# Routing attention and a tanh-shrink layer on one core: half of the first batch's up-projection in products of quarters

## The chip, the core and the metric

The kernel runs on one core of a Trainium2 chip. A core has a matmul engine (TensorE, "PE" in the profile, its weight loads "PEld"), a vector engine (VectorE, "DVE"), an activation engine (ScalarE, "ACT"), a general engine (GpSimd, "POOL") and a queue that only issues transfers (SyncE, "SP"). Each works through its own instructions in the order written and waits on semaphores. The metric is device time in microseconds, the median of several executions.

## The reference

Attention with routing: every query and key is assigned to the nearest of 16 centroids of its head, and a query sees only the keys of its own cluster. Then a two-layer block with the activation h - tanh(h).

```python
q, k, v: (4, 8, 768, 64)    centroids: (8, 16, 64)    w_in: (512, 2048)    w_out: (2048, 512)

q_assign = argmax(q_n . c_n)           k_assign = argmax(k_n . c_n)
mask   = q_assign[..., :, None] == k_assign[..., None, :]
scores = where(mask, q k^T / sqrt(64), -1e9)
attn   = softmax(scores)
x      = (attn v) as (4 * 768, 512)
h      = x @ w_in
out    = (h - tanh(h)) @ w_out
```

## The kernel before, in words

Everything is f32. Heads go in pairs (128 rows); a pair has two halves of 384 queries, and each half three steps of 256 keys. The list `steps` (L971) orders this work, 96 steps for 16 pairs: steps 0 to 11 are the first halves of batch 0's four pairs, 12 to 23 their second halves, and from 24 on come the pairs of batches 1 to 3 with both halves together, 24 steps (2 x HALF, HALF = 12) for a batch.

The main loop (L1103) writes one step after the other. For a step it emits the score matmuls of the step after (`begin`, L443; exps on ScalarE), the value matmuls of the step itself (`value`, L498) and some items of a "fill", the matmuls of the two-layer block of an earlier batch. What other engines have to do is kept in a list `todo`, and `between()` spreads it over the slots after the fill's items: the masks (`select`, L475: VectorE multiplies the exps by "key's cluster equals query's cluster", four operations, and POOL adds the weights up for the softmax's divisor, two operations of 128x768), the stages of a later pair (`turns`: transposes; `similar`; `route`, L358: the nearest centroid; `publish`: codes to DRAM), the chain that divides (`total`, `compact`, `invert`, `spread_out`, `scale`) and the makers.

A fill's items carry a weight, and the loop takes as many in each step as the weight's share of the fill's steps allows. Batch 0 is projected by `plain_items` (L665): first half in steps 12 to 23, second half in 24 to 47. For one half the up-projection has 16 items (`up`, L669, weight 2.6), each one chunk of 128 rows of h: 4 chunks of x times 2 half-widths of weights, 384 columns; ScalarE takes tanh from PSUM, VectorE subtracts. Then 12 items of the down-projection (`project`, L687, weight 3.4). An f32 product stands as two matmul instructions in the profile, so an item of `up` has 16.

Batches 1 to 3 use Strassen's scheme in Winograd's form (`strassen_items`, L834): x and the weights are cut into quarters, and 7 products of half the depth take the place of 8. The weights' seven combinations ("factors") are made once by `up_maker` and `down_maker` (L730, L751): sums on VectorE, then writes to DRAM by SP (`up_factors`, `down_factors`). The makers run as 44 entries of todo in steps 26 to 46. Factors come back as `stream` tiles of about 0.9 MB, three buffers, by `fetch_factors` (L786), two ahead. The combinations of x are made by `right_factors` (L822), 8 operations on VectorE for a batch, with 384 columns. Each of the 56 up-products (`up_product`, L840) is 8 matmul instructions on a PSUM tile of 384 columns; VectorE adds the products up to the quarters of h, then tanh on ScalarE and the subtraction on POOL (`shrink`).

PSUM tiles of the tag "f" (products, routing, divisors) share three buffers in turn. The weights w_in lie in a pool of their own on the right side of SBUF; `open_stream` (L799, at step 39) gives that place to the stream tiles and to a "den" tile, and `open_late` (L810, at step 48) gives the first batch's other tiles to the rest.

Of the kernel before, what the change touches and what calls it, by code (L numbers as in the profile page):

```python
# [39 lines left out]
P = 128  # L40
# [18 lines left out]
def kernel(  # L59
# [119 lines left out]
    def fast():  # L179
# [178 lines left out]
        def route(n: int):  # L358

            t = sims.pop(n)  # L360
            ps = ps_f.tile([P, TB], F32, name="pr", tag="f")
            for j in range(HCH):
                c = slice(j * P, (j + 1) * P)
                nc.tensor.transpose(out=ps[:, c], in_=t[:, c], identity=ident)  # L364
            G = HCH * 8
            pr = ps.rearrange("p (g c) -> p g c", c=C)
            shape = [P, G, C]
            places = down.unsqueeze(1).to_broadcast(shape)
            mx = rtp.tile([P, G], F32, name="mx")
            nc.vector.reduce_max(out=mx, in_=pr, axis=AX.X)  # L370
            top = rtp.tile(shape, F32, name="top")
            nc.vector.tensor_tensor(  # L372
                out=top, in0=pr, in1=mx.unsqueeze(2).to_broadcast(shape), op=ALU.is_ge
            )
            nc.vector.tensor_tensor(out=top, in0=top, in1=places, op=ALU.mult)
            code = codes[n] = codep.tile([P, 2, 2, 2, HCH], F32, name="code")
            nc.vector.reduce_max(
                out=code.rearrange("p i a h j -> p j (i a h)"),
                in_=top.rearrange("p (j g) c -> p j g c", j=HCH), axis=AX.X,
            )  # L380
# [238 lines left out]
        def spread_out(n: int, half: int):  # L619
            back = lists.pop((n, half))  # L620
            if joined(n):
                pool = late_pools.get("den", sump)
                dens[n, 1] = pool.tile([P, TB], F32, name="den")
                for i in range(2):
                    for h in range(2):
                        nc.sync.dma_start(
                            dens[n, i][h * D : h * D + D], back[i, h : h + 1].to_broadcast([D, TB])
                        )
                return
            for h in range(2):  # L630
                nc.sync.dma_start(
                    dens[n, half][h * D : h * D + D], back[h : h + 1].to_broadcast([D, TB])
                )
# [31 lines left out]
        def plain_items(half: int):  # L665
# [39 lines left out]
            if half == 0:  # L705

                order = [(s, i) for i in range(NQ4) for s in range(2)] + order[2 * NQ4 :]
            return [(2.6, 1, lambda between, f=f: up(f, between)) for f in sequence] + [
                (3.4, 1, lambda between, s=s, i=i: project(s, i, between)) for s, i in order
# [76 lines left out]
        def fetch_factors(n: int):  # L786

            if n < (B - 1) * PER:
                i = n % PER
# [7 lines left out]
        late_pools, diffs = {}, {}  # L797

        def open_stream():  # L799
# [4 lines left out]
            late_pools["den"] = cx.enter_context(  # L804
                tc.tile_pool(name="den_late", bufs=1, side="right", reuse_waits="tile")
            )
            for n in range(2):
                fetch_factors(n)

        def open_late():  # L810
            first.close()
            for name, bufs in (
                ("diff", 1), ("u", 2), ("s", 2), ("th", 2), ("g", 1), ("left", 1), ("du", 1),
                ("c", 4), ("raw", 2),
# [6 lines left out]

        def right_factors(b: int, c: int):  # L822

            if c == 0:
                diffs[b] = late_pools["diff"].tile([P, 3, CH, TB], F32, name="diff")
            d = diffs[b]
            x, y = xT[b * HP + c], xT[b * HP + CH + c]
# [6 lines left out]
        def strassen_items(b: int):  # L834
            base = (b - 1) * PER

            held = {}
            G, left1 = late_pools["G"], late_pools["S1"]

            def up_product(i: int, k_: int, between):  # L840
                which = PRODUCTS[k_]
                x = [xT[b * HP + c] for c in range(CD)]
                d = diffs[b]
                right = {
                    1: [x[c][:, 0] for c in range(CH)], 2: [x[CH + c][:, 0] for c in range(CH)],
                    3: [x[CH + c][:, 1] for c in range(CH)], 4: [d[:, 2, c] for c in range(CH)],
                    5: [d[:, 0, c] for c in range(CH)], 6: [d[:, 1, c] for c in range(CH)],
                    7: [x[c][:, 1] for c in range(CH)],
                }[which]
                if k_ == 0:  # L850
                    held[i] = (
                        late_pools["s"].tile([P, TB], F32, name="s"),
                        late_pools["u"].tile([P, 2, TB], F32, name="u"),
                    )
                s, u = held[i]
                g = G[:, i]
# [4 lines left out]
                def shrink(f: int, halves_=slice(0, 2)):  # L861
                    t = g[:, f, halves_]
                    th = late_pools["th"].tile([P, 2, TB], F32, name="th")[:, halves_]
                    nc.scalar.activation(out=th, in_=t, func=ACT.Tanh)  # L864
                    t, th = (x.rearrange("p a n -> p (a n)") for x in (t, th))
                    nc.gpsimd.tensor_tensor(out=t, in0=t, in1=th, op=ALU.subtract)  # L866

                ps = ps_f.tile([P, TB], F32, name="pu", tag="f")
# [8 lines left out]
                elif which == 2:  # L877
                    add(g[:, 0, 0], ps, s)
                    if i == HF - 1:
                        shrink(0, slice(0, 1))  # L880
# [5 lines left out]
                elif which == 4:  # L886
                    add(g[:, 1, 0], ps, u[:, 1])
                elif which == 5:
                    add(u[:, 0], ps, u[:, 0])
                    add(g[:, 1, 1], ps, u[:, 1])  # L890
                    shrink(1)
                else:
                    add(g[:, 0, 1], ps, u[:, 0])

                    shrink(0, slice(1 if i == HF - 1 else 0, 2))
                between()
                if k_ == len(PRODUCTS) - 1:

                    nc.gpsimd.tensor_tensor(out=left1[:, i], in0=g[:, 0, 1], in1=g[:, 1, 1], op=ALU.add)
                    nc.gpsimd.tensor_tensor(  # L900
                        out=g[:, 0, 1], in0=g[:, 0, 0], in1=g[:, 0, 1], op=ALU.subtract
                    )
                    streams.pop(base + i)
# [3 lines left out]
            def down_product(k_: int, j: int, between):  # L907
# [51 lines left out]

            return [  # L960
                (1.3, 1, lambda between, i=i, k_=k_: up_product(i, k_, between))
                for i in range(HF) for k_ in range(len(PRODUCTS))
            ] + [
# [11 lines left out]
        def before(n: int):  # L975
# [10 lines left out]
            yield lambda: route(n)  # L986
# [7 lines left out]
        ready = {}  # L994
# [68 lines left out]
        route(0)  # L1063
        turn(1, 0, nc.scalar)
# [13 lines left out]
        route(1)  # L1078
        begin(steps[0])
# [23 lines left out]
        for at, (n, half, s) in enumerate(steps):  # L1103
# [4 lines left out]
            if at == 4 * HALF - 9:  # L1108
                open_stream()
            if at in fills:  # L1110
                fill, over = fills[at][0](), fills[at][1]
                whole, spent, since = sum(it[0] for it in fill), 0.0, at
            if at == 2 * HALF:
                makers = [it for i in range(2) for it in up_maker(i)]
                makers += [it for i in range(2) for it in down_maker(i)]
# [71 lines left out]
            todo += [stages[i] for i in (5, 3, 4, 2) if i in stages]  # L1187
            todo += late
# [18 lines left out]
            light = [i for i in range(at, 4 * HALF - 2) if i % 3 and i % 6 != 1]  # L1207
# [8 lines left out]
            slots = max(sum(it[1] for it in now), 1)  # L1216
            place = iter(range(slots))
# [10 lines left out]
            if at in fills and "raw" in late_pools:  # L1228
# [10 lines left out]

        PRS = len(PRODUCTS)  # L1240
        tail = tail[:2] + tail[PRS : PRS + 2] + tail[2:PRS] + tail[PRS + 2 :]
# [218 lines left out]
```

## Time and profile before

| | |
|---|---|
| median of 5 runs | 982.39 us (982.27 to 982.99) |
| the profiled execution | 983.58 us |
| its span, first to last instruction | 981.8 us |
| TensorE busy | 971.4 us, 6456 matmul instructions |
| VectorE, ScalarE, POOL busy | 535.7, 316.5, 497.1 us |
| up-projection of batch 0, both halves (L676) | 86.3 us of TensorE, 512 instructions |
| up-projection of batches 1 to 3 (L871) | 134.9 + 102.3 us, 1344 instructions |
| granted TensorE clock | 1.0 |

Step k is found in the trace by its score matmuls (L451): step 20 begins at 160.1 us, step 24 at 202.4, step 25 at 208.8, step 36 at 288.8. In the page, busy time of PE is the time with at least one matmul in flight; matmuls overlap, so the mean duration of one (487 ns for L676) is longer than what it adds. The chain of work that ended last names, piece by piece, what the run's end waited for.

### The profile page before, as it was taken

What the parts mean: (1) busy time and instruction counts of PE and PEld (TensorE: products, weight loads), DVE (VectorE), ACT (ScalarE), POOL (GpSimd) and SP (SyncE); (2) the same over time, 40 slices, a digit from 0 to 9 for tenths busy, and PEclk for the clock granted to TensorE, in tenths of its full rate; (3) what the DMA queues carried; (4) which work ended last, traced back from release to release, by engine and by line L of the source; (5) the groups of instructions that cost most, each with busy time, mean ns of one, the idle gap of its engine ahead of it and who ended that gap; (6) DMA issues with size and microseconds to landing.
All of it is one profiled execution on the core that took longest, in us unless ns stands there. A gap on an engine that the chain in (4) does not pass through costs nothing.

```text
span 981.8 us, 16550 instructions
## 1 busy us (share of the span) xinstructions
PE 971.4 (99%) x6456; PEld 460.2 (47%) x6456; DVE 535.7 (55%) x1010; ACT 316.5 (32%) x484; POOL 497.1 (51%) x347
## 2 busy tenths in 40 slices
PE   8999999999999999999999999999999999999997
PEld 5433443344443334444455555444455555444664
DVE  6458656447566577647655457655755436543011
ACT  5576554233332333243422222333242121222000
POOL 1026334444445454677686345666688445466600
PEclk9999999999999999999999999999999999999999
DMA  7664453024565633463544646345344132233221
GB/s 206 180 188 142 151 143 94 30 73 132 154 205 166 173 116 110 148 195 99 185 147 168 184 137 200 110 151 157 115 159 137 59 118 98 82 111 129 104 103 35
DMA packets 113385, 132.47 MB, mean 135 GB/s; under 512 B 60388, under 2 KB 93076, under 8 KB 110612
## 3 DMA queue, kind: packets, MB, share of 16 engines
q1 hardware_dynamic: 106916, 109.81, 36.9%
q0 software_dynamic: 6240, 21.50, 6.4%
q8 instruction: 53, 0.87, 0.4%
q14 instruction: 32, 0.26, 0.1%
q10 hardware_dynamic: 144, 0.03, 0.0%
HBM read 110.14 MB, written 21.17 MB: 134 GB/s over the span
## 4 chain that ended last, share of the span: by engine, by line
PE 95%; DVE 2%; DMA 1%; ACT 1%; issue 0%; SPq 0%; ACTq 0%; DVEq 0%
PE pd L922 22%; PE pu L871 22%; PE sc L451 14%; PE av L505 13%; PE o L692 8%; PE h L676 8%; PE pt L332 2%; PE sim L351 1%; PE den L566 1%; DMA den<-back 1%; PE den L539 1%; PE den L520 1%; PE pr L364 1%; DVE e L483 1%; DMA row<-q_codes 0%
## 5 line engine op out<-in xcount | busy, mean ns | idle before, releaser
L496 POOL TENSOR_TENSOR sum<-sum,e 128x768 f32<-128x768 f32 x112 | 207.1, 1849 | 99.8 <-DVE e L483 93.9
L483 DVE SCALAR_TENSOR_TENSOR e<-row,code,sc 128x384 f32<-128x384 bf16 x336 | 186.1, 606 | 103.6 <-ACT sc L473 89.2
L473 ACT ACTIVATE sc<-sc 128x768 f32<-128x768 f32 x168 | 125.9, 792 | 215.9 <-PE sc L451 197.5
L922 PE MATMUL pd<-stream,G 128*64 128x256 f32 x1728 | 191.5, 379 | 0.0
L922 PEld LDWEIGHTS pd<-stream,G 128*64 128x64 f32 x1728 | 123.7, 137 | 67.0 <-issue 7.7
L451 PE MATMUL sc<-t,t 64*128 64x384 f32 x768 | 150.3, 509 | 0.6 <-ACT e L473 0.3
L505 PE MATMUL av<-e,vals 128*64 128x384 f32 x768 | 145.6, 498 | 0.3 <-DVE e L483 0.3
L871 PE MATMUL pu<-xT,stream 128*64 128x384 f32 x768 | 134.9, 488 | 0.7 <-DVE top L372 0.7
L866 POOL TENSOR_TENSOR G<-G,th 128x768 f32<-128x768 f32 (+1 forms) x51 | 87.2, 1722 | 94.0 <-ACT th L864 94.0
L871 PE MATMUL pu<-diff,stream 128*64 128x384 f32 x576 | 102.3, 488 | 0.0
L451 PEld LDWEIGHTS sc<-t,t 64*128 64x128 f32 x768 | 65.8, 186 | 75.3 <-issue 40.8
L492 POOL TENSOR_TENSOR sum<-e 128x768 f32<-128x768 f32 x28 | 54.3, 1941 | 77.9 <-DVE e L483 42.2
L871 PEld LDWEIGHTS pu<-xT,stream 128*64 128x64 f32 x768 | 54.1, 137 | 69.6 <-issue 61.9
L692 PE MATMUL o<-w_out,g 128*64 128x512 f32 x384 | 86.4, 594 | 0.0
L864 ACT ACTIVATE th<-G 128x768 f32<-128x768 f32 (+1 forms) x51 | 40.9, 806 | 141.2 <-DVE G L859 141.2
L676 PE MATMUL h<-xT,w_in 128*64 128x384 f32 x512 | 86.3, 487 | 0.0
L505 PEld LDWEIGHTS av<-e,vals 128*64 128x64 f32 x768 | 47.5, 136 | 82.5 <-issue 79.7
L871 PEld LDWEIGHTS pu<-diff,stream 128*64 128x64 f32 x576 | 40.4, 137 | 51.0 <-issue 44.7
L859 DVE TENSOR_TENSOR G<-pu,u 128x384 f32<-128x384 f32 x72 | 39.7, 552 | 43.5 <-PE pu L871 43.5
L676 PEld LDWEIGHTS h<-xT,w_in 128*64 128x64 f32 x512 | 36.4, 137 | 46.3 <-issue 45.1
L933 DVE SCALAR_TENSOR_TENSOR c<-pd,du 128x256 f32<-128x256 f32 x36 | 15.1, 420 | 66.5 <-PE pd L922 66.5
L692 PEld LDWEIGHTS o<-w_out,g 128*64 128x64 f32 x384 | 27.0, 137 | 50.1 <-issue 49.4
(131 smaller groups left out, 827.4 us busy)
## 6 DMA issues: line engine op xcount, KB each, us to landing
stream<-up_factors SPq DMA_DIRECT2D x24, 896.0 KB
stream<-down_factors SPq DMA_DIRECT2D x21, 1024.0 KB
raw<-in_moe_w_in_dram POOLq DMA_DIRECT2D x16, 512.0 KB, 5.1
raw<-in_moe_w_out_dram POOLq DMA_DIRECT2D x16, 512.0 KB, 4.1
again<-in_moe_w_in_dram SPq DMA_DIRECT2D x32, 256.0 KB
again<-in_moe_w_out_dram SPq DMA_DIRECT2D x32, 256.0 KB
x<-in_q_dram SPq DMA_DIRECT2D x32, 192.0 KB
x<-in_k_dram SPq DMA_DIRECT2D x32, 192.0 KB
```

Of the source, the lines that this page charges most:

```text
L451: nc.tensor.matmul(sc[i][:, h, 0:TB], lhsT=turned[n, 1][r].rearrange("p a n -> p (a n)")[:, j * P : (j + 1) * P], rhs=turned[n, 0][r, half ...
L473: nc.scalar.activation(out=out, in_=sc[i][:, :, 0:TB], func=ACT.Exp, scale=SCALE)
L483: nc.vector.scalar_tensor_tensor(out=e[:, h], in0=rows[n, half][:, h], scalar=codes[n][:, 1, j // HCH, h, j % HCH : j % HCH + 1], in1=sc[: ...
L492: nc.gpsimd.tensor_tensor(out=s, in0=pair[0], in1=pair[1], op=ALU.add)
L496: nc.gpsimd.tensor_tensor(out=s, in0=s, in1=pair[i], op=ALU.add)
L505: nc.tensor.matmul(avs[n, half][h * D : h * D + D], lhsT=vals[n][:, h, j], rhs=e[i][:, h], start=(j == 0), stop=(j == NCH - 1),)
L676: nc.tensor.matmul(h[r], lhsT=w_in[i][:, c, o * P : (o + 1) * P][:, r], rhs=xT[c][:, half], start=(c == 0), stop=(c == CD - 1),)
L692: nc.tensor.matmul(acc[sub][r], lhsT=gs[f % HF][:, f // HF, sub * P : (sub + 1) * P][:, r], rhs=w_out[f // FQ][:, f % FQ], start=(f == seq ...
L864: nc.scalar.activation(out=th, in_=t, func=ACT.Tanh)
L866: nc.gpsimd.tensor_tensor(out=t, in0=t, in1=th, op=ALU.subtract)
L871: nc.tensor.matmul(ps[r], lhsT=streams[base + i][:, c, k_, r], rhs=right[c], start=(c == 0), stop=(c == CH - 1),)
L922: nc.tensor.matmul(ps[r], lhsT=left(i)[:, r], rhs=t[:, i], start=(i == 0), stop=(i == HF - 1))
```

## The change

The up-projection of batch 0's second half (steps 24 to 35) goes through the same seven products as the later batches, with quarters of 192 tokens instead of 384: 56 products of 192 columns in place of 16 items of 384. For this

- `up_product` becomes part of `up_items`, which both use; the sums of the half's products go to VectorE, the subtraction of tanh to POOL;
- `right_factors` makes the combinations for this half too, at the start of step 24, 8 operations of 192 columns, before the first product is emitted; `start_without` puts four products that need none of them first;
- the items of the first maker move to steps 20 to 22, the second maker's to steps from 36 on;
- `open_stream` moves from step 39 to step 23, and eight more stream tiles are read; the "den" tile moves to another pool, and before step 48 a tile of `turnp0` serves;
- in steps 24 to 35 the masks of the next step (two entries of todo, three at the end of a pair, where the joined total stands between them) are emitted ahead of the step's fill items instead of between them;
- `route` is cut in two: the multiplication and the last maximum become `route_on`, emitted later in the same step;
- `project` of this half has weight 3.0 instead of 3.4.

```diff
+        def route_on(n: int):
+            top = tops.pop(n)
+            places = down.unsqueeze(1).to_broadcast([P, HCH * 8, C])
             nc.vector.tensor_tensor(out=top, in0=top, in1=places, op=ALU.mult)
...
-                pool = late_pools.get("den", sump)
-                dens[n, 1] = pool.tile([P, TB], F32, name="den")
+                if "den" in late_pools:
+                    dens[n, 1] = late_pools["den"].tile([P, TB], F32, name="den")
+                else:
+                    dens[n, 1] = turnp0.tile([P, 2, TB], F32, name="t0")[:, 0]
...
+            ups = [(2.6, 1, lambda between, f=f: up(f, between)) for f in sequence]
+            if half == 1:
+                ups = half_up_items(gs)
+            return ups + [
+                (3.4 if half == 0 else 3.0, 1, lambda between, s=s, i=i: project(s, i, between)) for s, i in order
             ]
...
+        def columns(b: int, c: int):
+
+            return xT[b * HP + c] if b else xT[c][:, 1].rearrange("p (a n) -> p a n", a=2)
...
         def right_factors(b: int, c: int):
             if c == 0:
-                diffs[b] = late_pools["diff"].tile([P, 3, CH, TB], F32, name="diff")
+                diffs[b] = (
+                    late_pools["diff"].tile([P, 3, CH, TB], F32, name="diff")
+                    if b else half_pools["diff"].tile([P, 3, CH, TB // 2], F32, name="diff")
+                )
             d = diffs[b]
-            x, y = xT[b * HP + c], xT[b * HP + CH + c]
+            x, y = columns(b, c), columns(b, CH + c)
...
+            return [
+                (1.3 * width / TB, 1, lambda between, i=i, k_=k_: up_product(i, k_, between))
+                for i in range(HF) for k_ in range(len(PRODUCTS))
+            ]
+
+        def start_without(items):
+            n = len(PRODUCTS)
+            return items[:2] + items[n : n + 2] + items[2:n] + items[n + 2 :]
+
+        def half_up_items(gs):
+            W = TB // 2
+            def quarter(i: int, f: int, t: int):
+                if i not in gs:
+                    gs[i] = gp.tile([P, 2, TB], F32, name="g")
+                return gs[i][:, f, t * W : (t + 1) * W]
+            def shrink(i: int, f: int, parts):
+                cols = slice(parts.start * W, parts.stop * W)
+                t = gs[i][:, f, cols]
+                th = thp.tile([P, TB], F32, name="th")[:, cols]
+                nc.scalar.activation(out=th, in_=t, func=ACT.Tanh)
+                nc.gpsimd.tensor_tensor(out=t, in0=t, in1=th, op=ALU.subtract)
+            return start_without(up_items(0, -HF, quarter, shrink, lambda i: None))
...
-            if at == 4 * HALF - 9:
+            if at == 2 * HALF - 1:
                 open_stream()
...
+            if at == 2 * HALF - 4:
+                makers = [it for i in range(2) for it in up_maker(i)]
             if at == 2 * HALF:
-                makers = [it for i in range(2) for it in up_maker(i)]
-                makers += [it for i in range(2) for it in down_maker(i)]
+                makers = [it for i in range(2) for it in down_maker(i)]
...
+            if 2 in stages:
+                if at < 2 * HALF or at >= 3 * HALF:
+                    stage = todo.pop()
+                    todo.append(lambda stage=stage: (stage(), route_on(routed.pop())))
+                else:
+                    todo.append(lambda: route_on(routed.pop()))
...
-            light = [i for i in range(at, 4 * HALF - 2) if i % 3 and i % 6 != 1]
+            light = [i for i in range(max(at, 3 * HALF), 4 * HALF - 1) if i % 6 != 1]
+            if at < 2 * HALF - 1:
+                light = list(range(at, 2 * HALF - 1))
...
+            if 2 * HALF <= at < 3 * HALF:
+                masks = 3 if half == 1 and s == NS - 1 else 2
+                for it in todo[:masks]:
+                    it()
+                todo = todo[masks:]
...
-            if at in fills and "raw" in late_pools:
+            if at == 2 * HALF or (at in fills and "raw" in late_pools):
                 for c in range(CH - 1 if at > 4 * HALF else 0, CH):
                     right_factors(b - 1, c)
```

## The prediction

> **What bounds the kernel now.** I read the page's busy shares and its chain first, then the chain and the timeline piece by piece around the place of the change, then the busy times of that stretch.
>
> ```profile
> span 981.8 us, 16550 instructions
> PE 971.4 (99%) x6456; PEld 460.2 (47%) x6456; DVE 535.7 (55%) x1010; ACT 316.5 (32%) x484; POOL 497.1 (51%) x347
> ...
> PE 95%; DVE 2%; DMA 1%; ACT 1%; issue 0%; SPq 0%; ACTq 0%; DVEq 0%
> ```
>
> TensorE is never out of work: 99% of the span, 95% of the chain. So a shorter matmul stream shortens the run one for one, and so does a wait put into it lengthen it; time freed on another engine is worth nothing by itself. The changed stretch is steps 24 to 35, 202.4 to 288.8 us. The windows (columns: stretch, length, busy time of PE, PEld, DVE, ACT, POOL with counts, granted clock, DMA share, GB/s) show PE full there and nobody else:
>
> ```profile
> 160.10:202.40 42.30, 42.30 (x215) 15.78 (x215) 22.81 (x37) 14.35 (x22) 18.16 (x14) 1.00 0.21 61
> 202.40:288.80 86.40, 86.40 (x530) 36.89 (x526) 55.72 (x87) 33.27 (x53) 38.75 (x21) 1.00 0.47 134
> 246.70:250.90 4.20, 4.20 (x28) 1.75 (x24) 2.19 (x4) 1.98 (x3) 1.00 (x1) 1.00 0.99 282
> 975.70:980.90 5.20, 0.00 (x1) 0.00 (x0) 0.42 (x1) 0.00 (x0) 0.00 (x0) 1.00 0.10 35
> 981.10:981.80 0.70, 0.00 (x0) 0.00 (x0) 0.00 (x0) 0.00 (x0) 0.00 (x0) 0.50 0.00 0
> ```
>
> **Part 1, the products.** What one matmul instruction costs in an unbroken stream is read from the chain's pieces (start, length, what):
>
> ```profile
> 183.69 6.87 PE o L692 x32
> ...
> 211.84 5.16 PE h L676 x32
> ...
> 491.72 6.91 PE pd L922 x64
> ```
>
> That is 214.7 ns at 512 columns, 161.25 at 384, 108.0 at 256: 0.417 ns per column between each two. The line goes on to 81.3 ns at 192 columns. Removed: 16 items of 16 instructions, 256 x 161.25 = 41.3 us. Added: 56 products of 8 instructions, 448 x 81.3 = 36.4 us. Gain 4.9 us, all of it on the path. The price at 192 columns is not in the trace. Its bounds: nothing lower than the straight line (81.3), nothing higher than the 256-column row (108.0, 48.4 us in all, a loss of 7.1). I take the line: 12 transposes with full 128-column weights pass in 1.46 us (the chain's piece at 285.19), 122 ns for each weight load with its matmul; a pair of products loads as many columns and has 162 ns for it.
> The Trainium skill's "TensorE: Matmul & The Clock Gate", section "Back-to-back issue gap", has 81 ns for 128 columns and 131 for 512 in a stream of load and matmul; a straight line between them gives, as an estimate, 89 ns at 192, and the saving would be 1.3 us. The trace's 214.7 at 512 columns shows that these f32 instructions do not follow that pair of figures, so the measured line stands.
>
> **Part 2, the first step.** Step 24 before, from the timeline:
>
> ```profile
> 203.84 0.85 PE L351 MATMUL sim<-t,bd 128*32 128x384 f32 x8
> ...
> 204.62 1.56 PE L451 MATMUL sc<-t,t 64*128 64x384 f32 x8
> ...
> 205.63 1.50 ACT L473 ACTIVATE sc<-sc 128x768 f32<-128x768 f32 x2 [0.40 <-PE sc L451]
> ...
> 206.11 2.80 PE L676 MATMUL h<-xT,w_in 128*64 128x384 f32 x16
> ...
> 206.46 2.19 DVE L483 SCALAR_TENSOR_TENSOR e<-row,code,sc 128x384 f32<-128x384 bf16 x4 [7.44 <-ACT sc L473]
> ...
> 207.75 3.69 POOL L496 TENSOR_TENSOR sum<-sum,e 128x768 f32<-128x768 f32 x2 [3.64 <-DVE e L483]
> ```
>
> After: the four masks end at 208.65 as here; behind them on VectorE come the 8 differences of right_factors, and only then the first sum (product 2 of output chunk 0). PE meanwhile runs the 4 products that need no difference, 4 x 0.65 us from 206.1, to 208.75. The fifth (product 6) needs a difference, and the third PSUM buffer, which that sum must free. What do the differences take? At 384 columns they follow each other every 0.48 us; with 192 columns less at VectorE's slope (a two-input operation takes 0.293 us at 128 columns, L251, and 0.55 at 384, L832; 192 columns less are 0.20 less) it is 0.29. Eight are 2.3 us. But they read and write SBUF alone, and beside POOL's sums such operations wait:
>
> ```profile
> 316.87 3.89 POOL L496 TENSOR_TENSOR sum<-sum,e 128x768 f32<-128x768 f32 x2 [1.84 <-DVE e L483]
> ...
> 317.68 3.50 DVE L638 TENSOR_TENSOR xT<-xT,den 128x384 f32<-128x384 f32 x2
> ...
> 373.03 0.55 DVE L832 TENSOR_TENSOR xT<-xT 128x384 f32<-128x384 f32 x1
> ```
>
> Two operations of 0.55 us that follow four masks take 3.50 here: the first until POOL's first sum is through, the second until its second is. Step 24 has the same picture (masks, then two sums from 207.75 on). So: first difference done at 209.8, second at 211.9 when the second sum is through, six more to 213.6, the sum of product 2 (0.35) to 213.9. PE waits from 208.75 to 213.9: 5.2 us, and all that is queued behind product 6 on PE (the scores of step 26, and with them every later step) waits as well. Bounds: 2.6 if POOL never holds VectorE up (the eight follow at once), 5.2 with both waits. I take 5.2, as the nearest row has both.
>
> **Part 3, the other eleven steps.** Per step, counted from the first score matmul (step 27: 228.6): exps +1.0 to +2.5, masks +1.9 to +4.1, value matmuls to +2.8, then 4 or 5 products of 0.65. The first sum runs at +4.1 to +4.5; the fourth product, at +4.8, needs the buffer it frees. Margin 0.3 us, so PE goes on. That is what the masks ahead of the sum cost: nothing while that margin holds, and one for one beyond it. In a routing step (25, 31) the transposes take the third buffer; there I count 0.25 us at step 31. In steps with a joined total (29, 35) the den matmuls come earlier, between the masks; the sums they need end at about +6.8 of the step before, 1.5 us ahead of them. I allow 0.6 us for all of this. Bounds: 0, and 2.5 (0.2 per step).
> VectorE's load over the stretch: 55.7, less 16 subtractions of 0.55, less the eight maker sums (11.4) and three of the second maker (3.6), plus 56 sums of 0.35 and the differences 2.3: about 54 of 82 us. POOL gets 16 subtractions of 1.0 (L866, 384 wide): 38.8 + 16 = 55 of 82. ScalarE gets 8 short copies. All below the bound on average; cover gone, each is paid as in part 2.
>
> **Part 4, what is moved.** The eight maker sums, 11.4 us with POOL's waits in them, go to steps 20 to 22; over steps 20 to 23 VectorE has 42.3 - 22.8 = 19.5 us free. A mask delayed there has 7 us until its value matmul. Cost 0; without that slack, up to the 11.4. The 28 up_factors writes (256 KB each, 7.3 MB) go with them; at the 282 GB/s of the best window 26 us, from about 166, and the last lands near 197. SP then passes, in order: the row of step 24 (178.8 before, now behind eight writes, about 185, needed at 192), the first two stream reads (0.9 MB, 3.3 us each, landing near 201 and 204 against use at 206.1 and 207.4), the q and k loads of pair 6 (198.4 before, needed five steps on), the next row. Cost 0; a first read up to 5 us late hides in the wait of part 2. Six more reads follow one chunk at a time, two chunks ahead, about 17 us before use. POOL's queue is passed by nothing but its own subtractions. The second maker starts at step 36 instead of in 279 to 350; it stays off the path. The split routing, the "den" tile in another pool, the pacing weight 3.0: 0, the order of work on PE is the same.
>
> **Sum.** -4.9 + 5.2 + 0.6 = +0.9 us on this execution's span of 981.8, with 1.8 around it (983.58 in all). That execution lies 1.2 above the median 982.39; on the median it is 983.3.
>
> **Rivals.** A, the sum above. Its own range is 982.7 to 985.2 (part 3 from 0 to 2.5).
> B, slower: the wait drops TensorE's clock. In the windows the granted clock is still 1.00 in the 5.2 us after the last matmuls and 0.50 at 981.1. My wait leaves the array empty for 4.9 us (the last matmul ends near 209.0), just short. If it decides from there, some microseconds of products run at half pace; at the start 14 warm-up matmuls take 4.99 us where later ones (1.46 for 6) say 3.2, so 1.8 lost: 985.1.
> The same page's Part 1 speaks against this change: an idle window of 3.4 us, free-running, halves the clock, and a busy one restores it. By it, a 4.9 us gap holds a whole window in 4 or 5 cases of 10, at 1.7 to 3.4 us: the sum would be 985.0 to 986.7 then.
> C: POOL's second sum does not get between the differences. The wait is 2.6 to 3.5: 980.7 to 981.6. Against it: L638 beside L496.
> D: the narrow products cost as much as 256 columns do (108 ns): 12 us more, 995.3. Against it: the straight line over three widths.
> E: no wait at step 24, the differences being through earlier, or PE having something else to do. Then 982.39 - 4.9 + 0.6 = 978.1. Against it: they stand behind masks that wait for that step's own exps.
>
> **How the numbers follow.** 0.2% is 2.0 us, about what a measurement of this kernel tells from no change. A 0.36, C 0.17, E 0.18, B 0.24, D 0.05. Faster (below 980.4): E 0.18 and the low end of C 0.03, 0.21. Slower (above 984.4): D 0.05, most of B 0.20, the top of A 0.08, 0.33. Same: 0.46. The range leaves out half of E and D: 978.0 to 987.5.
>
> **What would show it.** The product groups with 192 columns at about 0.65 us per 8 instructions. A hole of 5 us in PE before the fifth product of step 24, ended by VectorE, with two stretched differences beside POOL's sums. The half-1 up-projection (202.4 to 288.8) about 1 us longer. A clock of 0.5 after the hole means B; a hole ended by a stream read means that part 4 is wrong; many holes of some tenths mean that part 3 is.

## The result and the profile after

The changed kernel takes 985.18 us (median; 983.50 to 985.97) beside 982.83 us (982.01 to 983.53) for the kernel before: a ratio of 1.0023, 95% interval 1.0017 to 1.0029. It is 2.35 us slower; the forecast was 983.3 us, 0.9 above the 982.39 that it started from. The interval lies on both sides of the 0.2% that the prediction took as the least that can be told, so "the same" and "just slower" are both fair names for it. A later series of the same kernel gave 1.0012 (1.0003 to 1.0021); why two series of one kernel differ is part of the explanation.

The profiled execution of the changed kernel took 984.37 us. The page's first lines, then its share of the chain of waits, then the group of the products that need a difference:

```profile
span 982.6 us, 17051 instructions
PE 969.0 (99%) x6648; PEld 473.9 (48%) x6648; DVE 550.9 (56%) x1058; ACT 318.4 (32%) x493; POOL 514.0 (52%) x364
...
PE 97%; DVE 2%; ACT 0%; issue 0%; ACTq 0%
...
L887 PE MATMUL pu<-diff,stream 128*64 128x384 f32 (+1 forms) x768 | 121.4, 448 | 3.4 <-DVE diff L853 3.4
```

TensorE is busy 2.4 us less than before (971.4), and the span is 0.8 us longer. So idle time has come in, and the last line names 3.4 us of it: products that waited for VectorE's differences. The windows of the changed kernel show where (columns: stretch, length, then busy time of PE, PEld, DVE, ACT, POOL with counts, granted clock, DMA share, GB/s). The first is steps 20 to 23, the second steps 24 to 35, the others are pieces of step 24 and what follows it:

```profile
159.70:202.10 42.40, 42.40 (x217) 15.82 (x217) 34.30 (x45) 14.47 (x22) 18.16 (x14) 1.00 0.84 246
202.06:289.90 87.84, 84.41 (x724) 50.64 (x720) 55.94 (x125) 34.81 (x62) 53.63 (x38) 0.98 0.46 141
208.50:212.90 4.40, 0.97 (x10) 0.42 (x8) 4.33 (x8) 0.00 (x0) 2.48 (x2) 1.00 0.61 231
213.00:216.30 3.30, 3.30 (x12) 1.47 (x12) 1.48 (x6) 1.07 (x2) 0.00 (x0) 0.50 0.01 2
216.40:220.00 3.60, 3.60 (x35) 2.35 (x33) 2.79 (x6) 0.42 (x1) 3.00 (x2) 1.00 0.00 0
```

The first row is as long as before (42.3 us) with PE full, though VectorE now has 34.3 us of work there instead of 22.8. The third row is the hole: PE works 0.97 of 4.40 us. The fourth is what followed: PE is busy all the time, at a granted clock of 0.50, and does 12 instructions; the fifth row, at 1.00, has 35 in about the same time, most of them narrower. The timeline of the changed kernel shows how step 24 came to the hole:

```profile
205.73 2.82 PE L887 MATMUL pu<-xT,stream 128*64 128x192 f32 x32
...
206.07 2.19 DVE L488 SCALAR_TENSOR_TENSOR e<-row,code,sc 128x384 f32<-128x384 bf16 x4 [7.44 <-ACT sc L478]
...
207.37 3.69 POOL L501 TENSOR_TENSOR sum<-sum,e 128x768 f32<-128x768 f32 x2 [3.64 <-DVE e L488]
207.94 0.32 ACT L892 COPY t<-pu 128x192 f32<-128x192 f32 x1 [0.96 <-PE pu L887]
208.18 1.22 DVE L853 TENSOR_TENSOR diff<-xT 128x192 f32<-128x192 f32 x1
209.43 1.84 DVE L853 TENSOR_TENSOR diff<-xT,diff 128x192 f32<-128x192 f32 x1
211.19 0.34 DVE L853 TENSOR_TENSOR xT<-xT 128x192 f32<-128x192 f32 x1
...
211.42 0.55 PE L887 MATMUL pu<-diff,stream 128*64 128x192 f32 x4 [2.87 <-DVE diff L853]
...
212.52 0.55 PE L887 MATMUL pu<-diff,stream 128*64 128x192 f32 x4 [0.56 <-DVE diff L853]
...
212.94 0.62 DVE L882 TENSOR_TENSOR g<-pu,t 128x192 f32<-128x192 f32 x2
213.00 2.93 PE L456 MATMUL sc<-t,t 64*128 64x384 f32 x8
```

Four masks, then POOL's two sums, and beside them two differences of 1.22 and 1.84 us, where the third takes 0.34. PE runs out at 208.55, waits 2.87 us for the second difference and 0.56 us more for the sixth. The eight score matmuls behind it take 2.93 us; the same eight took 1.56 us in the kernel before (at 208.84 there).

To account for all of steps 24 to 35 I added up, by line, the time from the start of each TensorE instruction to the start of the next, from step 24's value matmuls to the first matmul of step 36's projection:

```
                                    stretch    products (instructions)
before                              87.85 us   42.59 (256)
after, the profiled execution       89.28
after, no half clock                87.68      42.33 (448)
differences first (experiment 1)    84.07      38.71 (448)
```

The first and the last row give the product change without a hole: 42.59 - 38.71 = 3.9 us saved. The hole takes 42.33 - 38.71 = 3.6 us of it back. What makes the stretch 89.28 in the profiled execution, 1.6 us more, is the half clock. Outside the stretch nothing moved: steps 13 to 24 stand a constant 0.38 us earlier than before, and everything from step 36 on a constant 1.05 us later, which is the stretch's own 1.43.

### The profile page after: what moved, and what is told of

It reads as the page before. It is cut to its first block, busy times and chain, and to the rows that moved or that the text cites. A ratio compares the mean times of both kernels' runs of the same rounds, so it can differ in the third digit from the quotient of the medians.

```text
span 982.6 us, 17051 instructions
## 1 busy us (share of the span) xinstructions
PE 969.0 (99%) x6648; PEld 473.9 (48%) x6648; DVE 550.9 (56%) x1058; ACT 318.4 (32%) x493; POOL 514.0 (52%) x364
## 4 chain that ended last, share of the span: by engine, by line
PE 97%; DVE 2%; ACT 0%; issue 0%; ACTq 0%
PE pu L887 25%; PE pd L983 22%; PE sc L456 15%; PE av L510 14%; PE o L700 8%; PE h L684 4%; PE pt L332 2%; PE sim L351 1%; PE den L525 1%; DVE e L488 1%; PE den L571 1%; PE pr L364 1%; PE den L544 1%; DVE diff L853 0%; PE pq L401 0%; PE sc L467 0%
## 5 line engine op out<-in xcount | busy, mean ns | idle before, releaser
L887 PE MATMUL pu<-xT,stream 128*64 128x384 f32 (+1 forms) x1024 | 159.6, 448 | 0.7 <-DVE top L371 0.7
L887 PE MATMUL pu<-diff,stream 128*64 128x384 f32 (+1 forms) x768 | 121.4, 448 | 3.4 <-DVE diff L853 3.4
L887 PEld LDWEIGHTS pu<-xT,stream 128*64 128x64 f32 x1024 | 72.0, 137 | 74.6 <-issue 64.8
L887 PEld LDWEIGHTS pu<-diff,stream 128*64 128x64 f32 x768 | 53.7, 137 | 59.9 <-issue 49.7
L994 DVE SCALAR_TENSOR_TENSOR du<-pd,du 128x256 f32<-128x256 f32 x27 | 11.3, 420 | 60.4 <-PE pd L983 60.4
L684 PE MATMUL h<-xT,w_in 128*64 128x384 f32 x256 | 42.9, 487 | 0.0
```

The source lines that it names most:

```text
L684: nc.tensor.matmul(h[r], lhsT=w_in[i][:, c, o * P : (o + 1) * P][:, r], rhs=xT[c][:, half], start=(c == 0), stop=(c == CD - 1),)
L887: nc.tensor.matmul(ps[r], lhsT=streams[base + i][:, c, k_, r], rhs=right[c], start=(c == 0), stop=(c == CH - 1),)
```

## The experiments

Two theories stood against each other after the result, both with a hole at step 24. By the first, the loss is the hole alone, and removing it must bring back about 3.6 us. By the second (the prediction's rival B), the hole has a tail: the halved clock behind it costs more, in some executions, and explains why the changed kernel's times spread over 2.5 us.

**1. The differences ahead of the masks in step 24.** The eight differences read only columns that are ready before the step, so nothing keeps them behind the masks but the order of VectorE's work.

```diff
+            if at == 2 * HALF:
+                for c in range(CH):
+                    right_factors(b - 1, c)
             if 2 * HALF <= at < 3 * HALF:
                 masks = 3 if half == 1 and s == NS - 1 else 2
...
-            if at == 2 * HALF or (at in fills and "raw" in late_pools):
+            if at in fills and "raw" in late_pools:
```

> The changed kernel with one thing moved: in step 24 the 8 differences of right_factors are emitted ahead of the step's masks instead of behind them. VectorE is idle before those masks (7.4 us before the change), and POOL has no sums yet. Theory 1 (the loss is the hole in TensorE at step 24, 3.9 us in the profile of after, and the halved clock behind it): hole and half clock both go, and what is left is -4.9 for the products and +0.8 for the other eleven steps: 4.1 us under the kernel before, about 978.7. Theory 2 (the loss lies in the other steps, and the hole only uncovers waits that would come anyway): the time stays 1 to 2.4 us above the kernel before.

Measured: 979.43 us (978.72 to 979.74) beside 983.10 for the kernel before; ratio 0.9959 (0.9945 to 0.9973). The chain of this kernel through step 24 (start, length, what) has no VectorE left in it, and the windows row of its steps 24 to 35 has a full PE and a whole clock:

```profile
206.18 2.75 PE pu L887 x32
...
208.97 0.87 PE pu L887 x8
209.84 1.49 PE sc L456 x8
```

```profile
202.40:286.50 84.10, 84.06 (x730) 50.81 (x726) 51.33 (x117) 35.65 (x64) 53.70 (x38) 1.00 0.50 151
```

So the hole, with what follows from it, is what made the change a loss: without it the change is worth 3.7 us, where 4.1 were expected. This version beats both kernels.

**2. The hole filled with idle matmuls.** Six warm-up matmuls (12 instructions of 256 columns, their result unused) ahead of the fifth product of step 24. The hole stays for the real work; the array is not idle in it.

```diff
-            for it in now:
+            for nth, it in enumerate(now):
+                if at == 2 * HALF and nth == 4:
+                    keep_warm(6)
                 it[2](between)
```

> The changed kernel with 12 warm-up matmul instructions (128x128 weights, 256 columns, result unused) emitted ahead of the fifth product of step 24: 2.6 us of TensorE work that waits for nothing, in the place where it sat idle from 208.55 to 211.42. The differences come no sooner, so the fifth product starts when it did. If the halved clock is a cause: the clock stays at 1.0 and the time falls to before -4.9 + 3.9 + 0.8, 0.2 us under the kernel before, and the runs scatter less than after's 2.5 us. If the halved clock costs nothing (or a fixed share of the loss lies elsewhere): the time stays 2.3 us above the kernel before.

Measured: 984.48 us (983.73 to 986.46); ratio 1.0018 (1.0009 to 1.0027), and a stretch of 88.85 us. The clock is 1.00 throughout in its profiled execution, yet the stretch is longer than in the changed kernel without a half clock. The timeline says why:

```profile
208.63 2.86 PE L302 MATMUL warm<-inverses 128*128 128x256 f32 x12
...
213.10 0.62 DVE L882 TENSOR_TENSOR g<-pu,t 128x192 f32<-128x192 f32 x2
213.51 0.87 PE L887 MATMUL pu<-diff,stream 128*64 128x192 f32 x8 [2.03 <-DVE g L882]
```

The warm-up took the third PSUM buffer, and the fifth product had to wait for VectorE's first sum to free one: a second hole, of 2.03 us, after the filled one. So this run does not tell the two theories apart. It does show what the prediction had assumed of the changed kernel, and what was not so there: a product that waits for a buffer, with the sum as its releaser, starts at 213.51, and in the changed kernel the product started at 211.42, before the sum.

**3. POOL's sums behind the differences.** In step 24, POOL's two sums are held back until the last difference is through. That takes away what stretches the differences and leaves them behind the masks.

```diff
+                    def add_up(s=s, pair=pair):
+                        for i in range(2):
+                            nc.gpsimd.tensor_tensor(out=s, in0=s, in1=pair[i], op=ALU.add)
+                    if holding:
+                        holding.append(add_up)
...
+            if at == 2 * HALF:
+                nc.gpsimd.tensor_copy(out=gate, in_=diffs[0][:, 2, CH - 1, 0:1])
+                for add_up in holding[1:]:
+                    add_up()
```

> The changed kernel, but in step 24 POOL's two sums wait for the last difference, so that no POOL operation runs beside the differences; the differences stand where they stood, behind the masks. If POOL's sums are what stretched the first two differences (1.22 and 1.84 us instead of 0.35): the second is done at 208.8 and the sixth at 210.0, the hole shrinks from 3.9 to about 1.3 us, the clock stays at 1.0, and the time is before -4.9 + 1.3 + 0.8, 2.8 us under. If the stretch had another cause (the place behind the masks, the in-place operand): the two stay long, the time stays 2.3 us above.

Measured: 981.19 us (980.47 to 981.51); ratio 0.9978 (0.9969 to 0.9987). Its timeline:

```profile
208.13 0.35 DVE L862 TENSOR_TENSOR diff<-xT 128x192 f32<-128x192 f32 x1
...
208.51 0.36 DVE L862 TENSOR_TENSOR diff<-xT,diff 128x192 f32<-128x192 f32 x1
...
209.01 0.55 PE L896 MATMUL pu<-diff,stream 128*64 128x192 f32 x4 [0.52 <-DVE diff L862]
...
210.12 0.55 PE L896 MATMUL pu<-diff,stream 128*64 128x192 f32 x4 [0.56 <-DVE diff L862]
...
210.81 7.50 POOL L505 TENSOR_TENSOR sum<-sum,e 128x768 f32<-128x768 f32 x4
...
217.28 1.46 DVE L380 TENSOR_TENSOR top<-top,down 128x384 f32<-128x384 f32 x1
```

The same two operations, at the same place, take 0.35 and 0.36 us instead of 1.22 and 1.84, and the hole is 0.52 + 0.56. So the stretching is POOL's doing. The stretch is 85.57 us, 1.5 over experiment 1: the hole's own size is as expected, the total fell 0.9 us short of the expected gain. The last two lines show one thing that the delay moved: POOL's sums, four in a row now, run until 218.3, and the routing's multiplication waits beside them for 1.46 us, where the kernel before has 0.56 for it. I did not separate what that costs.

**4, 7 and 8. The changed kernel again, for its clock.** No edit: a second series of times, and three more profiled executions.

> The changed kernel unaltered, beside the others on the same chip, for the scale: 2.3 us above the kernel before, one to two clock windows of 3.4 us at half rate behind the hole of step 24. If the half-rate stretch is not always the same length, its profile shows another start or another length than 212.96 and 3.41 us.

> The changed kernel again, for one more pair of time and clock record: without a half-rate stretch about 983.1, with one of 3.41 us about 984.4; if one of 6.8 us occurs, about 985.7.

> The same as the run before it: one more pair of time and clock record.

Measured: 984.27 us (983.00 to 986.02) in the series, and four profiled executions in all. Of the three new ones, the windows behind the hole, one fence for each (experiment 4, 7, 8):

```profile
213.00:216.00 3.00, 3.00 (x20) 1.38 (x22) 1.91 (x7) 1.50 (x2) 0.00 (x0) 1.00 0.03 10
216.10:218.50 2.40, 2.40 (x27) 1.64 (x23) 2.30 (x6) 0.00 (x0) 1.82 (x1) 1.00 0.00 0
```

```profile
213.00:216.00 3.00, 3.00 (x12) 0.97 (x10) 1.58 (x3) 1.59 (x2) 0.37 (x1) 0.50 0.00 0
216.10:218.50 2.40, 2.40 (x27) 1.45 (x23) 1.31 (x4) 0.00 (x0) 2.32 (x2) 1.00 0.00 0
```

```profile
213.00:216.00 3.00, 3.00 (x12) 1.49 (x12) 1.31 (x5) 0.41 (x1) 0.00 (x0) 0.50 0.05 15
216.10:218.50 2.40, 2.40 (x10) 0.77 (x8) 1.94 (x4) 1.08 (x2) 0.73 (x1) 0.50 0.00 0
218.60:222.00 3.40, 3.40 (x38) 2.49 (x35) 2.00 (x6) 0.00 (x0) 2.79 (x2) 1.00 0.00 0
```

One kernel, one hole, three outcomes. From the clock records of the four executions:

```
execution     half clock (us)              stretch 24-35    time
experiment 4  none                         87.68            983.09
experiment 7  212.62 to 216.04 (3.4)       89.34            983.49
first         212.96 to 216.38 (3.4)       89.28            984.37
experiment 8  211.71 to 218.53 (6.8)       90.31            985.90
```

One unit of half clock makes the stretch 1.6 to 1.7 us longer, two make it 2.6 longer. Experiment 7's time is lower than its stretch would have it (984.4 was expected with one unit) because it came to step 24 sooner, at 201.20 us; the four came there between 201.20 and 202.55.

The records suggest why the outcomes differ. Every stretch at full clock in them, up to a fall or between a recovery and the next fall, is a whole number of 3.413 us long: 61 of them (208.21 us) up to the fall in the first execution and in experiment 7, 60 (204.80 us) in experiment 8, and 224 (764.59 us) in all three from the recovery to the fall at the run's end. So the clock changes on a grid of 3.413 us, and the grid lies differently against the kernel in each execution. Counted back from the fall at the run's end, it also gives the units around the hole for executions in which the clock did not fall there. The unit with the least work in each:

```
execution     unit of the grid (us)   TensorE busy in it   clock in the next unit
experiment 8  208.29 to 211.71        0.74                 0.50
first         209.55 to 212.96        0.98                 0.50
experiment 7  209.21 to 212.62        1.50                 0.50
experiment 2  209.97 to 213.38        1.52                 1.00
experiment 4  207.61 to 211.02        1.58                 1.00
```

In experiment 4 a boundary of the grid cuts the hole in two, and the unit after it, to 214.43, has 2.01 us of work. Where the clock fell, it fell at the end of the unit that held most of the hole, and how the hole lies to the grid is the luck of each execution. That this decides is read off five records and not tested: no run moves the hole against the grid on purpose. Nor is there a sharp line in busy time: experiments 7 and 4 differ by 0.08 us, and a unit with 1.40 us at the end of experiment 9 (971.24 to 974.65) was not followed by a fall.

The other executions of the series have no such record, but each has its mean granted clock over the span. Half rate for 3.4 of 982 us lowers it by 0.0017, for 6.8 us by 0.0035. The eleven of experiment 4's series fall into line with that: four at 0.999 took 983.00 to 983.38 us, two at 0.997 took 984.14 and 984.27, and five at 0.996 took 984.29 to 986.02. In the first series all 22 lie at 0.998 or below: eleven at 0.996, which took 985.05 to 985.97 us, and eleven at 0.997 or 0.998, which took 983.50 to 985.32. One more execution on record beside that series, at 0.999, took 982.03 us. By this gauge the two series differ in how often the clock fell and for how long. The gauge is coarse: the kernel before, too, has mean clocks from 0.998 to 1.0.

**5. The hole filled in the product's own buffer.** The repair of experiment 2: eight idle matmuls (16 instructions of 192 columns, overwritten by the product that follows) into the fifth product's own PSUM tile, so that no buffer is taken.

```diff
                 ps = ps_f.tile([P, TB], F32, name="pu", tag="f")[:, 0:width]
+                if b == 0 and i == 0 and which == 6:
+                    for _ in range(8):
+                        nc.tensor.matmul(
+                            ps, lhsT=inverses[:, 0:P], rhs=inverses[:, 0:width], start=True, stop=True
+                        )
```

> As the run with the hole filled, but the idle matmuls (8 of 128x128 weights and 192 columns, 16 instructions, 2.6 us) write into the fifth product's own PSUM tile, which that product then starts anew, so that no third buffer is taken and the product starts when its difference is there, as in after. What is left idle is the 0.5 us between the product's two halves. The stretch from step 24 to step 36 should take 87.7 us, as in the profile of after that shows no half clock (85.85 would mean that the hole itself went, 89.3 that the half clock came all the same). If the half clock is what scatters after's runs over 3 us: this one's runs lie within 1.2 us, at 0.2 us under the kernel before. If not: they scatter as after's do, 1 to 2.4 us above.

Measured: 982.68 us (982.20 to 983.19) beside 982.78 for the kernel before; ratio 0.9998 (0.9989 to 1.0007); the stretch is 87.70 us. Timeline, and the same two windows as in the result:

```profile
208.56 2.87 PE L887 MATMUL pu<-inverses 128*128 128x192 f32 x16
...
209.52 1.85 DVE L853 TENSOR_TENSOR diff<-xT,diff 128x192 f32<-128x192 f32 x1
...
211.42 0.55 PE L892 MATMUL pu<-diff,stream 128*64 128x192 f32 x4
...
212.62 0.55 PE L892 MATMUL pu<-diff,stream 128*64 128x192 f32 x4 [0.65 <-DVE diff L853]
```

```profile
208.50:212.90 4.40, 3.75 (x26) 2.97 (x24) 4.33 (x8) 0.00 (x0) 2.58 (x2) 1.00 0.48 187
213.00:216.30 3.30, 3.30 (x26) 1.65 (x24) 2.21 (x7) 1.50 (x2) 0.01 (x1) 1.00 0.01 2
```

The first difference product starts at 211.42, as in the changed kernel: the useful work is as late as ever. But the array is not idle, the clock stays at 1.00, and the loss is gone, and with it the spread (1.0 us instead of 2.5 and 3.0 in the two series). This separates the two theories. The hole alone only cancels the saving (a ratio of 0.9998); the rest of the changed kernel's 2.35 us goes when the array is kept working, so it belongs to the clock.

**6. The differences first, and the masks spread over the step as before.** Experiment 1 with one more item of the change undone: the two or three masks of a step are no longer put ahead of its first product.

```diff
-            if 2 * HALF <= at < 3 * HALF:
+            if False:
                 masks = 3 if half == 1 and s == NS - 1 else 2
```

> The kernel with the differences ahead (979.4), and in steps 24 to 35 the masks back in the slots between the fill's items, as before the change. Theory 1 (the early masks cost nothing but the place they took from the differences in step 24): the same time, 3.7 us under the kernel before. Theory 2 (they are needed, since 4 or 5 short products leave VectorE no room): the second mask ends some 1.5 us later in each step, the scores of the step after wait for its PSUM buffer by 0.1 to 0.3 us in most of the eleven steps, and the time is 1 to 3 us above that, 1 to 2.5 us under the kernel before.

Measured: 992.23 us (991.92 to 992.95); ratio 1.0097 (1.0082 to 1.0113). That is 12.8 us more than experiment 1 by the medians, and 12.7 by the stretch (96.77 us); neither of the expected values was near. The timeline of one step and the waits over the stretch (engine and line, what it waited for, us in total, times, longest):

```profile
221.76 1.13 DVE L488 SCALAR_TENSOR_TENSOR e<-row,code,sc 128x384 f32<-128x384 bf16 x2
...
223.07 0.61 DVE L882 TENSOR_TENSOR g<-pu,t 128x192 f32<-128x192 f32 x2
...
223.60 1.13 DVE L488 SCALAR_TENSOR_TENSOR e<-row,code,sc 128x384 f32<-128x384 bf16 x2
...
224.88 0.92 PE L456 MATMUL sc<-t,t 64*128 64x384 f32 x4 [0.93 <-DVE e L488]
```

```profile
PE sc L456 <- DVE e L488: 5.1, 11, 0.9
...
PE pt L332 <- ACT t L339: 2.2, 2, 1.1
```

The masks now come in two pairs with product sums between them, and the next scores wait for the second pair: 11 waits of up to 0.9 us. The transposes wait twice, behind ScalarE. By line, the score matmuls take 25.80 us of the stretch instead of 19.38 in the kernel before, the value matmuls 19.73 instead of 17.68, the transposes 5.56 instead of 2.92. So the masks' place is no detail beside the narrow products: without it they would cost 9 us more than the wide ones they replace.

**9. The differences first, and the routing not split.** Experiment 1 with the multiplication and reduction of the routing joined to its first part again in steps 24 to 35.

```diff
-                if at < 2 * HALF or at >= 3 * HALF:
+                if True:
                     stage = todo.pop()
                     todo.append(lambda stage=stage: (stage(), route_on(routed.pop())))
```

> The kernel with the differences ahead, and route again in one piece in steps 24 to 35 (its multiplication and last maximum directly behind the first two operations). Theory 1 (the split is worth nothing, as the prediction has it, since VectorE is below its bound): the same as with the differences ahead, 3.7 us under the kernel before, within 0.3. Theory 2 (in the two routing steps, 25 and 31, the 1.1 us that come sooner on VectorE delay the sums of the products behind them, and these their PSUM buffers): up to 1 us at each, 2 us in all, 1.7 under the kernel before.

Measured: 980.25 us (979.40 to 980.86) beside 983.05; ratio 0.9971 (0.9960 to 0.9982), against 0.9959 in experiment 1: 2.8 us under the kernel before, between the two expectations. The stretch is 84.64 us instead of 84.07. The two intervals overlap, so that the split is worth anything is not shown by the times; the stretch of one profiled execution of each puts it at 0.6 us.

## Why the prediction was right, and where it was wrong

The forecast of 983.3 us lies 1.9 under the 985.18 measured, in its range and within 0.2% of it. But it was reached by two errors that partly cancel: its hole was 1.6 us too long, and the case that it took (A) had no clock in it. That it came as near as this is luck.

**Part 1, the products: right.** The price of 81.3 ns at 192 columns, read off the line through three wider rows, is what the chain shows (`1.30 PE pu L887 x16`, 81.3 ns each). Of the 4.9 us, 3.9 arrive. The difference is in the products' own rows: with the time to the following instruction counted in, they take 42.59 us for 41.3 of pure stream before and 38.71 for 36.4 in experiment 1. Of this 1.0 us, 0.3 are two late starts in experiment 1: the fifth product of step 24 by 0.21 us, behind VectorE's first sum, and one by 0.11 us at 255.29, in a routing step. The rest lies in the passages between products and other work: the products now stand in 16 unbroken runs where there were 12, and a run takes 0.05 to 0.21 us more than its instructions alone. Rival D, products at the price of 256 columns, is excluded. So is the estimate from "Back-to-back issue gap" in the Trainium skill's "TensorE: Matmul & The Clock Gate" (89 ns): no run here shows it for these products.

**Part 2, the wait: right place and cause, wrong size.** PE dried up at 208.55 (forecast 208.75), two differences were stretched beside POOL's two sums, and the first was through at 209.40 and the second at 211.27 (forecast 209.8 and 211.9). The step that failed is "The fifth (product 6) needs a difference, and the third PSUM buffer, which that sum must free." Product 6 started at 211.42 and the sum only at 212.94: it did not need the sum. Two of the four products before it are read by VectorE's sums alone, which had not run, so with three buffers it must have had one that ScalarE's copies of the two "product 1"s (the second at 207.94) had read out. The buffers are thus not handed on strictly in turn, as I had described them; in experiment 1 the same product was released by the sum, and what decides was not found. Experiment 2, where something else took that buffer, shows the wait that the prediction described. Going by the differences alone, with the prediction's own times, the second half of the product would have had to wait for the sixth difference at 211.9 + 4 x 0.29 = 213.1, and the hole would have come to about 4.0 us (213.1 less 208.75, less 0.33 for the first half product) instead of 5.2. Measured: 3.4 by the waits, 3.6 by the accounting.

The mechanism was the right one: experiment 3 moves POOL's sums away and the differences take 0.35 us. The Trainium skill has a rule for it that the prediction did not draw on, in "SBUF — State Buffer", section "SBUF: two separate sides": VectorE operations with two SBUF inputs and GpSimd operations that read SBUF share a pair of ports as an exclusive lock, held for the whole instruction. The trace agrees: 1.22 and 1.84 us beside POOL, 0.34 to 0.36 without it, and VectorE's first difference ends at 209.40, just behind POOL's first sum (about 209.2, half of the two sums' 3.69 us).

**Part 3, the other eleven steps: near.** I allowed 0.6 us. No wait of PE for a sum shows in them; what there is are the 0.11 us in a routing step (I had counted 0.25 there) and the passages above. That the masks ahead of the sum "cost nothing" was so, but I had set only their cost: experiment 6 shows that they are worth 12.8 us to the narrow products. The split of the routing, taken as 0, is 0.6 us by the stretch and 0.9 by the medians, and not clear of the noise.

**Part 4, what is moved: right.** All of it at zero. VectorE took 11.5 us more in steps 20 to 23 (34.30 for 22.81) with PE full in both. On SP's queue, behind the up_factors writes, the row of step 24 went out 2 us later than I had put it (185), and the first stream read where I had it (197):

```profile
186.97 0.86 SPq L414 DMA_DIRECT2D row<-q_codes  x1
...
196.80 0.86 SPq L807 DMA_DIRECT2D stream<-up_factors  x1
```

Neither is waited for at step 24; the offset to the kernel before stays at 0.38 us until the hole.

**A against B: the wrong choice.** Rival B, 985.1 us, is what came. I put it behind A because at the end of the run the clock still stood at 1.00 for 5.2 us after the last matmul, and my hole was empty for 4.9, "just short". That row was no threshold. On the grid described under experiments 4, 7 and 8 it reads otherwise: in the kernel before, the unit from 974.20 to 977.61, in which the last matmuls ended, still had 1.50 us of work, the next had none, and the clock fell at that one's end, 981.02. In the three executions that show a fall, it came 2.7 to 4.9 us after PE dried up (experiment 8: 209.03 to 211.71; experiment 7: 207.69 to 212.62), and the hole was shorter than I had made it, with 0.55 us of work in its middle. In the first execution and in experiment 7 the hole was already over, or nearly, when the clock fell. The cost is near B's 1.8 us: 1.6 to 1.7 by the stretch with one unit, 2.6 with two. By the times, the level without a half clock is 983.2 (the four runs at 0.999 in experiment 4, beside 983.1 for the kernel before), and 984.3 to 986.0 at the mean clock of two units (0.996). That B's sum meets the median to 0.1 us is chance, since it holds the same long hole as A's.

The rule that the prediction quoted from "TensorE: Matmul & The Clock Gate", Part 1 (a free-running window of 3.4 us, half rate after an idle one), fits better than my row did: the half rate lasts 3.41 or 6.83 us, one or two of its windows, is exactly 0.50, and comes in some executions and not in others. In one point the measurement is harsher than the rule as I used it. I had asked that a whole window lie in the empty time. The 3.41 us before the fall were not empty: TensorE was busy for 0.73 us of them in experiment 8, 0.98 in the first execution (209.55 to 212.96) and 1.50 in experiment 7.

C (the second sum does not get between the differences) and E (no wait) did not occur. E's condition, the differences being through earlier, is what experiment 1 builds; E put it 4.3 us under the kernel before, and it is 3.7.

With the buffer step right, the sum would have been -4.9 + 4.0 + 0.6 = -0.3 us, about the 0.9998 of experiment 5; there too the errors cancel, since the first and last terms came to -3.9 together instead of -4.3, and the hole to 3.6. The rest of the 2.35 us needed the clock.

## What to carry to other kernels

When an engine's order puts the operations that feed the next product behind others that nobody waits for yet, look first at whether they could simply run earlier: here that was three lines, and it turned a loss of 2.35 us into a gain of 3.7. Price a hole on TensorE of about 3 us or more at its own length plus what a fall of the clock costs in some executions (here 1.6 to 2.6 us), and take a spread of times that the old kernel did not have as a sign of it. Before counting on a short two-input VectorE operation, see what POOL runs at that moment: the operation may take as long as what is left of POOL's.

## What the hardware showed that I had not expected

The half clock comes in units: 3.41, 3.41 and 6.83 us in the three executions that had it. In experiment 8 the second unit ran although PE had been busy for 3.03 of the 3.41 us of the first (211.71 to 215.12); in the first execution and in experiment 7 a first unit with PE busy throughout (3.41 us) was also the last. So a wholly busy unit ended the half clock twice, and one with 0.38 us of idle time did not end it once; three records do not show where between them the line lies.

Experiment 2's times spread over 2.7 us (983.73 to 986.46) though its one profiled execution, 984.35 us, had a whole clock. Its mean clocks go with the times (0.999 for 983.73 to 984.48 us, 0.997 or 0.998 for 984.66 to 986.46), so its second hole of 2.03 us may do the same; but 0.998 also occurs in the kernel before, at 982.7. No record of one of its slower executions was taken, and this stays open.
